# Token halves in the output tiles, gates on a whole bank, and earlier squares and gate logits, in a fused SSM and expert kernel

## The chip, the cores and the metric

The kernel runs on one core of a Trainium2 chip. The metric is the device time of one execution in microseconds; it is read as the median of repeated runs. A separate execution is profiled by the hardware, and its trace gives the views that are quoted here.

## The reference

The output mixes two branches of the same tokens with a gate per token. L is 2048 tokens, D is 576 channels.

```python
x = A_u
g = sigmoid((x * gate_w).sum(-1, keepdims=True))
a = S4(x)      # K[d,l] = Re sum_n C[d,n] exp(dt A l) dt B[d,n]; y = conv(x, K) + x * Dskip
b = PEER(x)    # below
return g * a + (1 - g) * b

# PEER: 32 heads, 64 x 64 = 4096 experts
q  = x @ w_q                                # 32 heads, two halves of 128
s1 = q[..., :128] @ k1.T; s2 = q[..., 128:] @ k2.T   # 64 scores each
# two best of s1 and of s2 give four candidates, the two best of these are the experts
g   = softmax(top_s)                        # over the two
act = gelu(x @ u[top_e])                    # one number per token, head, choice
out = sum over heads and choices of g * act * v[top_e]
```

## The kernel before

**Layout.** The 2048 tokens stand in 16 tiles of 128. The convolution is done by a two-step Fourier transform in matmuls. PEER is done densely: the activations of every token with all 4096 experts are computed (`a` matmuls) and kept in DRAM as `g_d`, and the choice of experts enters as a sparse matrix of gates.

**Stages.** In the *token stage* TensorE computes scores (`s`, from folded keys `whl` and tokens `xb`) and activations (`a`, from `uhl` and `xb`); the taps K of the convolution are generated beside them (`kP` and `kb` matmuls, CS, e, ex and Y on the other engines), and `u_stage1` does the first Fourier step of the tokens (`u` matmuls from `uh`). VectorE takes the best scores from the `s` banks (`m`, `i`). In the *frequency stage* (`freq`), which begins when all taps are stored, `ksb` is loaded, `k_stage1` transforms the taps (`k` matmuls, `k1o`, stored to `sk_d`), `products` multiplies the spectra (`pr`, `pi`, `pv`, `tt`, `vf`, `vo`), and `gating` makes gates and places from the best scores. `v_norm` runs there too: it squares the 32 blocks of value rows for a common scale, and then, in the same loop with the same tiles `vn`, multiplies 16 tiles of tokens by `gate_w` on GpSimd and sums them on ScalarE into the gates `gA`. `v_work` splits the values into f16 high and low parts `vhl` once the scale is known. The *output stage* goes through the 16 tiles in `ORDER` (0, 15, 1, 14, ...).

**One output tile.** `prep` loads the tile's activations from `g_d` in two parts `gl` and puts them through gelu. `onehot` builds, for each of four quarters of the tile's tokens, one-hot matrices `A`, `Be` and the gated `Bg` on VectorE. TensorE multiplies them into banks `S`, and VectorE multiplies `gl` by these banks. The result is split into f16 high and low weights `wh`, and 192 `o` matmuls (32 blocks of experts, three products of high and low parts, two halves of the channels) give the tile's output. `y_part` adds the convolution (`y` matmuls, `ya`); `ya*db` is computed on GpSimd.

**What sets the order.** The program is written by generators under a clock of its own: `clock[0]` counts the matmuls' cost, and each engine has a `free` time that grows by a cost formula per operation. A generator yields until what it needs is ready by that clock (`ready`), or until a buffer is free (`need`, `take`, `free` on tags such as `slot`, `wb`, `sc`). The order in which instructions stand in each engine's queue is thus decided when the program is built, from estimated times; on the chip each engine works through its queue in order and waits for semaphores. Which engine does a split or a copy also follows from the estimated `free` times. All helpers record through one line, so the profile shows L134 for every operation of VectorE, ScalarE and GpSimd, L214 for matmuls and L205 for DMAs on SyncE; the tiles' names tell them apart. The nine buffers `slot` hold `gl` and `wh` in the output stage, 9 KB per partition each.

The lines of `prep` that the prediction's steps concern, with the loads, the four multiplies per quarter, and the weights made at the end:

```python
dma(gl[h], g_d[t][:, 16 * h:16 * h + 16])
...
for h in range(2):
    gv = gl[h].rearrange("p b (r n) -> p b r n", r=2)[:, :, :, n0:n0 + 8]
    V.tensor_tensor(out=gv, in0=pv[:, 16 * h:16 * h + 16], in1=gv, op=OP.mult)
...
yield from split(fl(h[0][:, bs]), fl(h[1][:, bs]), fl(src), s_wg)
```

Of the kernel before, what the change touches and what calls it, by code (L numbers as in the profile page):

```python
# [24 lines left out]
D = 576  # L25
# [113 lines left out]
def body(ctx: ExitStack, tc: tile.TileContext, xT, au, par, logdt, dskip, gatew, wq, kT, uT, vv,  # L139
# [841 lines left out]
    def gating(c):  # L981
# [81 lines left out]
    def u_stage1():  # L1063
# [31 lines left out]
        load(0)  # L1095
        for p in range(NT):
# [4 lines left out]
            h = uf.tile([128, 2, D], F16, tag="uh", name=f"uh{p}", bufs=2)  # L1101
# [22 lines left out]
        while ended[0] < NT:  # L1124
            yield 1
# [139 lines left out]
    def freq():  # L1265
# [14 lines left out]
        spawn(v_norm(), 40)  # L1280
# [115 lines left out]
    def v_norm():  # L1396
        ld = {}

        def load(b):
            a = ff.tile([128, D], F32, tag="vn", name=f"vn{b}", bufs=2)  # L1400
            if b < 32:
                dma(a, vv[128 * b:128 * b + 128])
            else:
                au_load(a, b - 32)
            ld[b] = a
# [3 lines left out]
        for b in range(48):  # L1409
            if b + 1 < 48:  # L1410
                load(b + 1)
            a = ld.pop(b)
            yield from ready(a)
            ju = ff.tile([128, D], BF16, tag="ju", name=f"vj{b}")
            if b < 32:
                S.activation(ju, a, AF.Square, accum_out=vsum[:, b:b + 1])
            else:
                G.tensor_mul(a, a, gw)
                yield from ready(a)
                S.activation(ju, a, AF.Copy, accum_out=gA[:, b - 32:b - 31])  # L1420
            yield 2
            if b != 31:
                continue
            V.tensor_reduce(out=nut[:, 2:3], in_=vsum, axis=AX, op=OP.add)
            yield from ready(nut)
            tag = side()
            yield from need(tag)
            p = bank(tag, "pvn")
            mm(p[:, 0:1], onesb, nut.bitcast(BF16)[:, 5:6], True, True, 0.05)
            yield from ready(p)  # L1430
            sv.extend(root_scale(p[:, 0:1], 1.02))
            free(tag, sv[0])
            vnormed.append(1)
            del p
# [60 lines left out]
    def prep(t):  # L1495
# [9 lines left out]
        yield from ready(*gl)  # L1505
        for h in range(2):
            for b0 in (0, 8):
                g = gl[h][:, b0:b0 + 8]
                S.activation(g, g, AF.Gelu_apprx_tanh)
        for q in range(4):  # L1510
# [20 lines left out]
            del pbs, pS, pv  # L1531
# [4 lines left out]
        h = []  # L1536
        for z in range(2):
            yield from need("slot")
            h.append(slot([32, 128], F16, f"wh{t}_{z}"))
# [300 lines left out]
```

## Time and profile before

| | before |
|---|---|
| median of 3 runs | 1456.58 us (1456.38 to 1456.81) |
| profiled execution | 1458.63 us, its span 1456.8 us, mean granted clock 0.998 |
| busy: PE, DVE, ACT, POOL | 98%, 84%, 53%, 36% of the span |
| last `u` matmul of the token stage | starts at 633.6 us |
| `k` matmuls | 678.7 to 744.2 us |
| products and the transposes of the places | `pv` from 771.3, `tr` to 939.7 us |
| first and last `S` matmul | 954.8 and 1400.0 us |
| first and last `o` matmul | 995.3 and 1452.8 us |

PE is TensorE's matmuls, PEld its weight loads, DVE VectorE, ACT ScalarE, POOL GpSimd and SP SyncE. Busy time of an engine says nothing of what the kernel waits for; that is read from PE's idle time and from who ended it. In the views a row of a group has its count, its busy time, the mean of one in ns, and the idle time of the engine just before it with what ended that; a row of the timeline has start, length, engine, operation and, in brackets, the idle time before it.

### The profile page before, as it was taken

To read this page: it belongs to the slowest core of one execution; us is meant where nothing else is said; L and a number is where in the kernel's file an instruction comes from. 1 tells how busy PE (TensorE), PEld (TensorE's weight loads), DVE (VectorE), ACT (ScalarE), POOL (GpSimd) and SP (SyncE) were. 2 spreads that over 40 slices of the span, in tenths; PEclk is the share of its full clock that TensorE was granted. 3 is DMA by queue.
4 is the path that set the end of the run, shared out by engine and by line. 5 is a ranking of instruction groups with operands and counts; after the bars stand their busy time and mean duration, and the time that the engine had idled before them with its cause. 6 is when DMAs were issued, how large, how long until landed. Compare 5 with 4: busy or idle time off the path is not lost.

```text
span 1456.8 us, 36814 instructions
## 1 busy us (share of the span) xinstructions
PE 1430.8 (98%) x14103; PEld 853.9 (59%) x14105; DVE 1221.0 (84%) x4569; ACT 776.0 (53%) x1304; POOL 521.4 (36%) x510
## 2 busy tenths in 40 slices
PE   7999999999999999999999999999899999999998
PEld 3445445555454445455555444447687887888787
DVE  6898889889877996885989898689998988998860
ACT  6346776796685776834556564576333224323310
POOL 0335357536446446210237999623000100110100
PEclk9999999999999999999999999999999999999999
DMA  8235223442434432269486776787343432342400
GB/s 306 77 112 172 88 80 109 126 138 72 129 106 124 116 104 92 62 211 292 157 304 216 266 250 214 255 265 228 130 122 110 140 120 98 125 148 67 157 9 17
DMA packets 134352, 215.44 MB, mean 148 GB/s; under 512 B 10912, under 2 KB 79904, under 8 KB 127776
## 3 DMA queue, kind: packets, MB, share of 16 engines
q1 hardware_dynamic: 134080, 213.01, 45.3%
q8 instruction: 111, 1.82, 0.5%
q14 instruction: 65, 0.53, 0.1%
q10 hardware_dynamic: 96, 0.07, 0.0%
HBM read 141.74 MB, written 71.30 MB: 146 GB/s over the span
## 4 chain that ended last, share of the span: by engine, by line
PE 85%; DVE 5%; DMA 2%; ACT 1%; issue 0%; POOL 0%; SPq 0%; DVEq 0%; POOLq 0%
PE o L214 25%; PE s L214 22%; PE a L214 22%; PE S L214 4%; PE kb L214 2%; PE wb L214 2%; PE pr L214 2%; DMA vn<-in_au_dram 1%; PE y L214 1%; PE kP L214 1%; PE k L214 1%; DVE i L134 1%; PE pv L214 1%; PE u L214 1%; DVE vhl L134 1%; DVE m L134 1%
## 5 line engine op out<-in xcount | busy, mean ns | idle before, releaser
L214 PE MATMUL o<-vhl,wh 128*128 128x288 f16 x3072 | 389.2, 287 | 0.0
L214 PE MATMUL s<-whl,xb 128*128 128x512 f16 x1536 | 365.0, 379 | 0.0
L214 PE MATMUL a<-xb,uhl 128*128 128x512 f16 x1536 | 359.5, 379 | 0.2 <-DVE go L134 0.2
L214 PEld LDWEIGHTS <-wh 128*128 128x128 f16 x3072 | 296.8, 98 | 77.5 <-issue 3.7
L214 PEld LDWEIGHTS <-xb 128*128 128x128 f16 x1792 | 170.6, 98 | 208.5 <-issue 14.3
L214 PEld LDWEIGHTS <-uhl 128*128 128x128 f16 x1536 | 147.1, 98 | 176.3 <-issue 3.2
L134 DVE FIND_INDEX8 i<-m,s 128x8 uint32<-128x64 f32 x1024 | 206.9, 226 | 0.0
L134 ACT ACTIVATE wh<-gl,s_wg 128x1024 f16<-128x1024 f32 x64 | 69.0, 1137 | 203.6 <-DVE gl L134 203.6
L134 DVE MAX8 m<-s 128x8 f32<-128x64 f32 x1024 | 146.4, 217 | 27.1 <-PE s L214 26.6
L134 POOL TENSOR_TENSOR CS<-CS,ex 128x512 f32<-128x512 f32 x72 | 97.9, 1389 | 147.6 <-DVE ex L134 146.2
L134 POOL TENSOR_TENSOR ya<-ya,db 128x576 f32<-128x576 f32 x16 | 31.8, 1995 | 320.3 <-DVE Bg L134 159.2
L134 ACT ACTIVATE go<-a,i_a 128x512 f32<-128x512 f32 x92 | 61.5, 682 | 89.1 <-PE a L214 63.9
L134 DVE TENSOR_TENSOR gl<-S,gl 128x256 f32<-128x256 f32 x256 | 90.3, 416 | 13.5 <-PE S L214 10.1
L134 POOL TENSOR_TENSOR e<-aN,rt 128x512 f32<-128x512 f32 x72 | 83.1, 1174 | 49.9 <-PE kb L214 43.8
L134 DVE SCALAR_TENSOR_TENSOR wh<-gl,s_wg,wh 128x1024 f16<-128x1024 f32 x64 | 91.1, 1455 | 11.3 <-ACT wh L134 11.3
L134 DVE TENSOR_TENSOR Bg<-Be,vals 128x1024 f16<-128x1024 f16 x128 | 91.7, 758 | 2.2
L134 ACT ACTIVATE gl<-gl 128x1024 f32<-128x1024 f32 x64 | 63.4, 1044 | 34.1 <-DMA gl<-g_d 34.1
L214 PE MATMUL S<-Bg,A 128*128 128x64 f16 x2048 | 73.6, 194 | 6.4 <-DVE Bg L134 6.4
L214 PEld LDWEIGHTS <-A 128*128 128x128 f16 x2048 | 71.4, 98 | 11.4 <-DVE Bg L134 4.9
L134 DVE TENSOR_TENSOR A<-iota_a,vals 128x2048 f16<-128x2048 f16 x64 | 77.9, 1218 | 0.0
L134 DVE MATCH_VALUE_LOAD i<-m,s 128x8 f32 x1024 | 76.3, 75 | 0.1
L214 PE MATMUL s<-wrem,xb 128*128 128x512 f16 x256 | 76.2, 379 | 0.0
(206 smaller groups left out, 2156.6 us busy)
## 6 DMA issues: line engine op xcount, KB each, us to landing
g_d<-go SPq DMA_DIRECT2D x128, 256.0 KB, 2.4
gl<-g_d SPq DMA_DIRECT2D x32, 1024.0 KB, 5.5
wq<-in_wq_dram SPq DMA_DIRECT2D x16, 1152.0 KB, 5.6
su_d<-us SPq DMA_DIRECT2D x32, 288.0 KB, 2.6
sk_d<-k1o SPq DMA_DIRECT2D x32, 288.0 KB, 3.7
vn<-in_vv_dram SPq DMA_DIRECT2D x32, 288.0 KB, 4.1
ui<-su_d SPq DMA_DIRECT2D x16, 576.0 KB, 4.0
ki<-sk_d SPq DMA_DIRECT2D x16, 576.0 KB, 5.5
```

The costliest lines, as they stand in the source:

```text
L134: return f(*a, **k)
L214: T.matmul(o, l, r, start=start, stop=stop)
```

## The change

Four edits are made together.

- A half of a tile is now 64 tokens with all 32 blocks of experts, where it was 128 tokens with 16 blocks. The identity that transposes the places takes its columns in another order, so that quarters 0 and 1 are the first 64 tokens. The load of a half takes 64 of 128 tokens from each row of `g_d`.
- VectorE multiplies `gl` by a whole bank `S` in one instruction of 512 elements, in place of two of 256.
- The weights of a half are made by a generator of its own, `weights`; that of the first half starts after the second quarter.
- `v_norm` keeps only the squares and runs in the token stage, from `u_stage1`, in place, with one buffer; `uh` gets one buffer in place of two. The gate logits become `gate`, which starts 4 us after the frequency stage's loads, where `v_norm` started after 40.

```diff
-                    mm(p[64 * hh:64 * hh + 64, 64 * r:64 * r + 64], x, i[:, 64 * hh:64 * hh + 64], True, True,
-                       0.12 if r == 2 else 0.04)
+                    mm(p[64 * hh:64 * hh + 64, 64 * r:64 * r + 64], x,
+                       i.rearrange("p (h r n) -> p r h n", h=2, r=2)[:, hh], True, True, 0.12 if r == 2 else 0.04)
...
         load(0)
+        spawn(v_norm())
         for p in range(NT):
...
-            h = uf.tile([128, 2, D], F16, tag="uh", name=f"uh{p}", bufs=2)
+            h = uf.tile([128, 2, D], F16, tag="uh", name=f"uh{p}", bufs=1)
...
-        while ended[0] < NT:
+        while ended[0] < NT or not vnormed:
             yield 1
...
-        spawn(v_norm(), 40)
+        spawn(gate(), 4)
         spawn(gating(0), 20)
...
     def v_norm():
+        for b in range(32):
+            a = uf.tile([128, D], F32, tag="vn", name=f"vn{b}", bufs=1)
+            dma(a, vv[128 * b:128 * b + 128])
+            yield from ready(a)
+            S.activation(a, a, AF.Square, accum_out=vsum[:, b:b + 1])
+            yield 9
+        V.tensor_reduce(out=nut[:, 2:3], in_=vsum, axis=AX, op=OP.add)
...
+    def gate():
...
+        for t in range(NT):
+            if t + 1 < NT:
+                load(t + 1)
+            a = ld.pop(t)
             yield from ready(a)
+            ju = ff.tile([128, D], BF16, tag="ju", name=f"gj{t}")
+            G.tensor_mul(a, a, gw)
+            yield from ready(a)
+            S.activation(ju, a, AF.Copy, accum_out=gA[:, t:t + 1])
             yield 2
...
-        gl = [slot([16, 128], F32, f"gl{t}_{h}") for h in range(2)]
+        gl = [slot([32, 64], F32, f"gl{t}_{h}") for h in range(2)]
         for h in range(2):
-            dma(gl[h], g_d[t][:, 16 * h:16 * h + 16])
+            dma(gl[h], g_d[t][:, :, 64 * h:64 * h + 64])
...
+            h = q // 2
             for hb, pS in enumerate(pbs):
-                n0 = 16 * q + 8 * hb
-                pv = pS.rearrange("p (k r b) -> p b r k", r=2, b=32)
-                for h in range(2):
-                    gv = gl[h].rearrange("p b (r n) -> p b r n", r=2)[:, :, :, n0:n0 + 8]
-                    V.tensor_tensor(out=gv, in0=pv[:, 16 * h:16 * h + 16], in1=gv, op=OP.mult)
-                free("wb", *gl)
+                n0 = 16 * (q % 2) + 8 * hb
+                gv = gl[h].rearrange("p b (r n) -> p b r n", r=2)[:, :, :, n0:n0 + 8]
+                V.tensor_tensor(out=gv, in0=pS.rearrange("p (k r b) -> p b r k", r=2, b=32), in1=gv, op=OP.mult)
+                free("wb", gl[h])
...
+            if q == 1:
+                for z in range(2):
+                    yield from need("slot")
+                    wh.append(slot([32, 128], F16, f"wh{t}_{z}"))
+                spawn(weights(t, 0, wh, gl[0]))
...
+        spawn(weights(t, 1, wh, gl[1]))
+
+    def weights(t, h, wh, g):
+        yield from ready(g)
+        for b in (slice(0, 16), slice(16, 32)):
+            hi, lo = (x[:, b, 64 * h:64 * h + 64] for x in wh)
+            src = g[:, b]
...
+                yield from split(hi, lo, src, s_wg)
             yield 0.3
-        free("slot", h[1])
-        free("slot", h[1])
-        st[t] = h
+        free("slot", wh[1])
+        if h:
+            while t not in half:
+                yield 0.3
+            st[t] = wh
+        half.append(t)
```

On VectorE, at the third output tile (the number in a name is a buffer's running number), from `Bg` of its second quarter on. Before, the order of the program is this; behind its last row stand the four multiplies `gl` of the first quarter, then `A`, `Be` and `Bg` of the third.

```order
L134 TENSOR_TENSOR Bg_1_13451<-Be_1_13449,vals 128x1024 x2
L134 SCALAR_TENSOR_TENSOR wh_1_13434<-gl_0_13021,s_wg,wh_0_13433 128x1024
L134 SCALAR_TENSOR_TENSOR vhl_12950<-vhl_12951,sci,vhl_12950 128x576
L134 SCALAR_TENSOR_TENSOR wh_1_13434<-gl_0_13021,s_wg,wh_0_13433 128x1024
L134 SCALAR_TENSOR_TENSOR wh_1_13434<-gl_1_13022,s_wg,wh_0_13433 128x1024
L134 SCALAR_TENSOR_TENSOR vhl_12951<-vs,sci,vhl_12951 128x576
L134 SCALAR_TENSOR_TENSOR ya_13355<-y_0_0_13574,iuk,ya_13355 128x288
L134 SCALAR_TENSOR_TENSOR ya_13355<-y_0_1_13579,iuk,ya_13355 128x288
L134 SCALAR_TENSOR_TENSOR wh_1_13434<-gl_1_13022,s_wg,wh_0_13433 128x1024
L134 SCALAR_TENSOR_TENSOR vhl_12951<-vs,sci,vhl_12951 128x576 x2
L134 SCALAR_TENSOR_TENSOR ya_13360<-y_1_0_13584,iuk,ya_13360 128x288
L134 SCALAR_TENSOR_TENSOR ya_13360<-y_1_1_13589,iuk,ya_13360 128x288
```

After the change the same stretch, up to `Bg` of the third quarter, is this:

```order
L134 TENSOR_TENSOR Bg_1_13402<-Be_1_13400,vals 128x1024 x2
L134 SCALAR_TENSOR_TENSOR vhl_12475<-vs,sci,vhl_12475 128x576
L134 SCALAR_TENSOR_TENSOR wh_1_13219<-gl_1_13002,s_wg,wh_0_13218 128x16x64
L134 SCALAR_TENSOR_TENSOR ya_13366<-y_0_0_13536,iuk,ya_13366 128x288
L134 SCALAR_TENSOR_TENSOR ya_13366<-y_0_1_13541,iuk,ya_13366 128x288
L134 SCALAR_TENSOR_TENSOR ya_13371<-y_1_0_13546,iuk,ya_13371 128x288
L134 SCALAR_TENSOR_TENSOR ya_13371<-y_1_1_13551,iuk,ya_13371 128x288
L134 TENSOR_TENSOR gl_0_13387<-S_0_0_13575,gl_0_13387 128x64x8
L134 TENSOR_TENSOR gl_0_13387<-S_0_1_13592,gl_0_13387 128x64x8
L134 TENSOR_TENSOR A_2_13635<-iota_a,vals 128x2048
L134 TENSOR_TENSOR Be_2_13637<-iota_b,vals 128x1024
L134 TENSOR_TENSOR Bg_2_13639<-Be_2_13637,vals 128x1024 x2
```

One wh and one vhl stand between the two Bg where four of each stood; the other three wh of the tile before are ahead of this stretch.

On ScalarE, in the token stage at the first step of `u_stage1`. Before:

```order
L134 ACTIVATE uh_963<-us,sci 128x576
L134 ACTIVATE go_2_3_1003<-a_2_3_965,i_a 128x512
L134 ACTIVATE vals<-m_0_4_807 128x4x16
L134 ACTIVATE idx<-i_0_4_808 128x4x16
L134 ACTIVATE uhl_893<-us_790,sci 128x512 x2
```

After:

```order
L134 ACTIVATE uh_965<-us,sci 128x576
L134 ACTIVATE vn_918,vsum<-vn_918 128x576
L134 ACTIVATE go_2_3_1006<-a_2_3_967,i_a 128x512
L134 ACTIVATE vals<-m_0_4_807 128x4x16
L134 ACTIVATE idx<-i_0_4_808 128x4x16
L134 ACTIVATE uhl_893<-us_790,sci 128x512 x2
```

A square (`vn`) now stands ahead of the copy of an activation bank (`go`); 32 of them follow each other in this way, the last ahead of the thirteenth of 16 `uh`.

TensorE's instructions are the same in kind, size and number. Between `y` and the third tile's third quarter of `S` its queue has two quarters of `S` and 54 `o` matmuls, where it had 60; the fourth quarter of the second tile stands ahead of the first `o` matmul, where 18 `o` stood ahead of it.

More of the change, by code (lines that the diff above doesn't have):

```diff
@@ L1396, in v_norm @@
     def v_norm():
-        ld = {}
[L1399 to L1405, printed above, removed]
+        for b in range(32):
[4 more added lines that the diff above has]
+            yield 9
@@ new lines, in v_norm, with load @@
+        V.tensor_reduce(out=nut[:, 2:3], in_=vsum, axis=AX, op=OP.add)
+        yield from ready(nut)
+        tag = side()
+        yield from need(tag)
+        p = bank(tag, "pvn")
+        mm(p[:, 0:1], onesb, nut.bitcast(BF16)[:, 5:6], True, True, 0.05)
+        yield from ready(p)
+        sv.extend(root_scale(p[:, 0:1], 1.02))
+        free(tag, sv[0])
+        vnormed.append(1)
+    def gate():
+        ld = {}
+        def load(t):
+            ld[t] = ff.tile([128, D], F32, tag="vn", name=f"xg{t}", bufs=2)
+            au_load(ld[t], t)
@@ L1532, in prep @@
+            del pbs, pS
             if q < 2:
                 oh[q + 2] = onehot(t, q + 2)
+            if q == 1:
[3 more added lines that the diff above has]
+                spawn(weights(t, 0, wh, gl[0]))
         if t != ORDER[-1]:
             spawn(prep(ORDER[ORDER.index(t) + 1]))
[L1536 to L1539, printed above, removed]
@@ L1549, in prep @@
             else:
-                yield from split(fl(h[0][:, bs]), fl(h[1][:, bs]), fl(src), s_wg)
+                yield from split(hi, lo, src, s_wg)
             yield 0.3
-        free("slot", h[1])
-        free("slot", h[1])
-        st[t] = h
+        free("slot", wh[1])
[4 more added lines that the diff above has]
+        half.append(t)
+    half = []
     yt = {}
```

44 lines of the change are left out of this document (8 added, 36 removed).

## The prediction

> **What bounds the kernel now.** I read the page first, then busy time by windows, PE's waits, and the timeline around the one large wait.
>
> ```profile
> PE 1430.8 (98%) x14103; PEld 853.9 (59%) x14105; DVE 1221.0 (84%) x4569; ACT 776.0 (53%) x1304; POOL 521.4 (36%) x510
> ```
>
> PE is busy for 1430.8 us, 98% of the span of 1456.8. The change leaves PE's multiset of instructions as it is, so time can only move in the other 26.0 us, plus what a lower clock costs. The windows say where these lie; a row has the stretch, its length, the busy time of PE, PEld, DVE, ACT and POOL (with counts), the granted clock, the DMA share and GB/s.
>
> ```profile
> 0.00:50.00 50.00, 40.69 (x307) 20.31 (x309) 31.07 (x86) 29.91 (x51) 12.55 (x13) 1.00 0.78 262
> 250.00:300.00 50.00, 50.00 (x544) 25.48 (x543) 41.74 (x126) 36.74 (x56) 31.89 (x26) 1.00 0.42 131
> 450.00:500.00 50.00, 48.35 (x498) 24.01 (x493) 42.57 (x188) 36.10 (x55) 19.73 (x18) 1.00 0.37 111
> 850.00:900.00 50.00, 48.29 (x456) 22.85 (x449) 46.49 (x280) 25.83 (x71) 48.67 (x44) 1.00 0.58 192
> 1000.00:1050.00 50.00, 45.06 (x503) 34.30 (x501) 48.22 (x68) 23.21 (x26) 10.43 (x6) 0.93 0.57 182
> 1150.00:1200.00 50.00, 50.00 (x610) 40.53 (x608) 46.52 (x73) 12.14 (x13) 2.82 (x2) 1.00 0.41 133
> ```
>
> The start loses 9.3 us (50 − 40.69) and the change touches none of it. From 1100 on PE is full although DVE works 46.52 of 50, so cheaper DVE work there buys nothing by itself. The large loss is in 1000 to 1050, where the output tiles begin: PE idles 4.94 us and the granted clock falls.
>
> ```profile
> PE S L214 <- DVE Bg L134: 6.4, 4, 4.6
> PE u L214 <- DVE uh L134: 1.9, 2, 1.4
> PE kb L214 <- issue: 1.6, 1, 1.6
> PE pi L214 <- DVE i L134: 1.3, 1, 1.3
> ```
>
> ```profile
> 1023.00:1028.00 5.00, 0.43 (x4) 0.12 (x3) 4.97 (x11) 0.78 (x1) 0.00 (x0) 0.96 0.96 343
> 1028.00:1032.00 4.00, 3.64 (x40) 2.84 (x41) 3.96 (x8) 0.00 (x0) 0.00 (x0) 0.50 0.43 180
> 1032.00:1036.00 4.00, 4.00 (x27) 2.71 (x24) 3.05 (x8) 0.00 (x0) 0.00 (x0) 0.69 0.00 0
> ```
>
> S matmuls wait for the one-hot product Bg four times, 6.4 us, the longest 4.6. Behind the longest the clock stands at 0.50 for 4 us and 0.69 for 4 us: 4 × 0.50 + 4 × 0.31 = 3.2 us of matmul time. So DVE's lag in this stretch costs 6.4 + 3.2 = 9.6 us.
>
> ```profile
> 1007.72 3.50 DVE L134 TENSOR_TENSOR Bg<-Be,vals 128x1024 f16<-128x1024 f16 x2
> 1008.82 3.67 POOL L134 TENSOR_TENSOR ya<-ya,db 128x576 f32<-128x576 f32 x2
> 1011.83 2.15 PE L214 MATMUL y<-yz,tf 128*32 128x288 f32 x32
> 1018.37 4.25 POOL L134 TENSOR_TENSOR ya<-ya,db 128x576 f32<-128x576 f32 x2 [5.88 <-DMA ya<-in_au_dram]
> 1019.39 3.85 DVE L134 SCALAR_TENSOR_TENSOR vhl<-vs,sci,vhl 128x576 f16<-128x576 f32 x2
> 1027.19 1.29 DVE L134 TENSOR_TENSOR Bg<-Be,vals 128x1024 f16<-128x1024 f16 x2
> 1027.94 0.23 PE L214 MATMUL S<-Bg,A 128*128 128x64 f16 x1 [4.57 <-DVE Bg L134]
> ```
>
> DVE ended Bg of the third tile's second quarter at 1011.2 and of its third quarter at 1028.5: 17.3 us of unbroken work, while PE needed it at 1023.1. Beside POOL's products DVE steps stretch: a pair of Bg takes 3.50 us at 1007.72 and 1.29 at 1027.19.
>
> **The change part by part.** *Gates on a whole bank.* Per tile 16 multiplies of 256 elements become 8 of 512.
>
> ```profile
> L134 DVE TENSOR_TENSOR gl<-S,gl 128x256 f32<-128x256 f32 x256 | 90.3, 416 | 13.5 <-PE S L214 10.1 <-ACT gl L134 3.5
> L134 DVE TENSOR_TENSOR CS<-CS,kP 128x512 f32<-128x512 f32 x19 | 13.1, 687 | 0.7
> L134 DVE SCALAR_TENSOR_TENSOR wh<-gl,s_wg,wh 128x1024 f16<-128x1024 f32 x64 | 91.1, 1455 | 11.3 <-ACT wh L134 11.3
> L134 DVE TENSOR_TENSOR A<-iota_a,vals 128x2048 f16<-128x2048 f16 x64 | 77.9, 1218 | 0.0
> L134 DVE TENSOR_TENSOR Be<-iota_b,vals 128x1024 f16<-128x1024 f16 x64 | 46.2, 721 | 0.0
> L134 DVE TENSOR_TENSOR Bg<-Be,vals 128x1024 f16<-128x1024 f16 x128 | 91.7, 758 | 2.2
> L134 DVE SCALAR_TENSOR_TENSOR ya<-y,iuk,ya 128x288 f32<-128x288 f32 x32 | 15.0, 510 | 0.0
> ```
>
> The nearest 512-element product out of a bank takes 687 ns, so a tile pays 8 × 0.687 = 5.5 instead of 16 × 0.416 = 6.7 us; over 16 tiles DVE loses 18.6 us of work. From 1100 on that lies beside a full PE and is worth nothing; it counts where DVE is late.
>
> *Token halves.* The 192 transposes read the identity's columns in another order, in the same number and size: 0. The weights wh of a half are split after two quarters. Per tile the same four splits run, so their sum stays; they move ahead of the later one-hots. In the new order, between Bg of the third tile's second and third quarters DVE has one vhl, one wh, four ya, two gl, one A, one Be and two Bg: 1.06 + 1.46 + 4 × 0.51 + 2 × 0.69 + 1.22 + 0.72 + 2 × 0.76 = 9.4 us against the 17.3 measured (vhl's mean below). Most of these have room, so what counts is the chain from y on.
>
> ```profile
> 1056.86 3.67 PE o L214 x30
> 1060.53 0.97 PE S L214 x32
> L134 DVE SCALAR_TENSOR_TENSOR vhl<-vhl,sci,vhl 128x576 f16<-128x576 f32 x19 | 19.7, 1060 | 0.8 <-issue 0.8
> ```
>
> An o matmul is 3.67 / 30 = 0.122 us and a quarter of S 0.97. From y's start the new PE order has y (2.1), 12 o, S, 6 o, S, 36 o, then the third quarter: 2.1 + 54 × 0.122 + 2 × 0.97 = 10.6 us. On DVE the first quarter's S ends at 2.1 + 1.5 + 1.0 + about 0.3 = 4.9; two gl (1.4) and A, Be, 2 Bg (3.5) end at 9.8. The four ya end at 4.6 and delay nothing. DVE is ahead by 0.8. Two products of POOL may each stretch a step by 1.1 (3.50 against 1.29 for the pair): then 12.0, a wait of 1.4, and up to 1 us again at the fourth quarter, where 24 o and S (3.9) stand against 4.9 of DVE. So 0 to 2.4 remain; I take 0.8. None comes near the 4.57 that went before the clock's fall, so the 3.2 us of clock go too. The first two tiles, which hold the other S waits, get shorter gl work and no gate product of POOL (next part), so I take all 9.6 off.
>
> *Loads of gates.* A half's load is now 4096 runs of 256 bytes instead of 128 runs of 8 KB.
>
> ```profile
> gl<-g_d SPq DMA_DIRECT2D x32, 1024.0 KB, 5.5
> g_d<-go SPq DMA_DIRECT2D x128, 256.0 KB, 2.4
> DMA to landing us min/median/max: 7.5/8.5/12.4
> L134 POOL TENSOR_TENSOR vn<-vn,gw x16: 1395/1412/1846, 838.7 to 959.4; 128x576 f32<-128x576 f32 x16
> ```
>
> No load of before has runs of 256 bytes. The third row is ksb's: 18 × 128 = 2304 runs of 512 bytes, 1.18 MB, 8.5 us. By bytes a half (1.05 MB) takes 7.6 us at that rate; by runs, (8.5 − 2.4) / (2304 − 512) = 3.4 ns a run (2.4 us and 512 runs are g_d's store), 4096 runs take 2.4 + 3584 × 0.0034 = 14.6. I take 7.6: gl and ksb move 190 and 139 bytes per ns, nearer to each other than their counts of runs (18 fold). What hides it: in the new order a tile's first S stands 84 o or more behind the last S of the tile before, whose end releases the load: 84 × 0.122 = 10.3 us, plus S itself, and now only the first half and its two gelus must be there. Cost 0; without that cover it is a rival below. The Trainium skill, DMA: Bandwidth & Descriptors, Specifications, puts line rate at runs of 512 bytes or more and says that below this the engine does read-modify-write; no run of before shows it.
>
> *Squares and gate logits.* 32 loads and squares of value rows move from 715–835 to the token stage, 16 gate products to the start of the frequency stage.
>
> ```profile
> L134 ACT ACTIVATE vj<-vn 128x576 bf16<-128x576 f32 x48 | 33.1, 689 | 11.2 <-DMA vn<-in_vv_dram 8.9 <-POOL vn L134 2.2
> L134 ACT ACTIVATION_READ_ACCUMULATOR vj<-vn 128x1 f32 x48 | 9.7, 202 | 0.0
> L205 SPq DMA_DIRECT2D vn<-in_au_dram x64: 310/419/2223, 825.6 to 955.7; - x64
> L134 ACT ACTIVATE uh<-us,sci x16: 759/764/785, 92.1 to 626.4; 128x576 f16<-128x576 f32 x16
> L134 ACT ACTIVATE go<-a,i_a 128x512 f32<-128x512 f32 x92 | 61.5, 682 | 89.1 <-PE a L214 63.9 <-issue 22.4 <-DMA g_d<-go 2.3
> ```
>
> ACT gets 32 × (0.689 + 0.202) = 28.5 us between 92 and about 510, some 3.4 per 50 us beside 36.74; the last square stands ahead of the last four uh, so the stage does not wait for it. Each is queued ahead of go, us and the CS steps on ACT; a late load (8.9 us over 8 times, 1.1 each) holds these, and PE through full banks. Bounds: 0, since go already waits for PE 63.9 us, and 12 us if one in three of 32 pays 1.1. I take 0.8. The load of square n+1 on SP waits for square n, 9 us older, so nothing on SP stands behind it. On SP the gates' 64 loads leave 826 to 956 and stand among the stores of the taps' spectrum and of g_d at the start of the frequency stage; each waits for a product two tiles older, and these stores wait behind it. What needs the stores (a ring of three, the products) runs beside s matmuls that fill PE: 0, within the ±1.5 below. One uh buffer instead of two makes ACT wait for u matmuls issued 12 us before: 0. Earlier squares open the vhl work from about 750 instead of 833, but tiles 3 to 7 still wait for their pools: DVE has 13 vhl steps after the products now, 14 before. The gate products (1.41 each on POOL) leave 838 to 961, where POOL was busy 48.67 of 50; PE does not wait for POOL there, so this gives DVE undisturbed steps and nothing of its own. The sigmoid's table load leaves the output start. The waits of pi, u and kb I leave as they are (a shuffle of ±1.5).
>
> **The sum.** −9.6 + 0.8 + 0.8 = −8.0 us. The profiled execution took 1458.63 us, 1.83 around its span and 2.05 above the median 1456.58; the same difference on the median gives 1448.6.
>
> **The rivals.** *The wait stays.* POOL's ya products fall on the third tile's one-hots and DVE is 3 us or more later than reckoned (its backlog of vhl has a margin of about 6 us ahead of y). PE then waits 3 to 4 us again. Whether the clock falls lies between 1.6 us (kb's wait, 1.00 in 450 to 500) and 4.57. By the Trainium skill, TensorE: Matmul & The Clock Gate, Part 1, about 3.4 us of idleness halves it; the 4.57 agrees, and no row shows the border itself. With 3.5 + 3.2 back, 1448.6 − 0.8 + 6.7 = 1454.5, within the bound below. For it: the second pair of ya products began 6.5 us behind y (1018.37 against 1011.83), where the third quarter's one-hots now stand. Against: 9.4 us of work where 17.3 stood.
>
> *The squares hold ACT in the token stage* (the other side): at 12 us or more of late banks, 1448.6 + 11.2 = 1459.8, slower. It decides from about one square in three delaying a go that a bank waits for. Against: ACT has 13 us free in each 50.
>
> *Runs of 256 bytes bound the stage.* A tile takes PE 192 × 0.122 + 4 × 0.97 + half a y, 28.4 us. At 3.4 ns a run, two halves hold the engines 27.9 us per tile; a DMA share of 0.41 is 11.6, of which the old gl loads (2.1 of 3.8 MB at 133 GB/s) were over half, so 5 stay: 33 against 28.4, +4.5 for 14 tiles, some 1510. It decides from (28.4 − 5) / 8192 = 2.9 ns a run. Against: by bytes the same row gives 7.6 us a half. The Trainium skill's rule on short runs, cited above, would have it come out this way.
>
> **How the numbers follow.** A measurement here tells about 0.2% (2.9 us) from no change: 1453.7 to 1459.5 is the same. Forecast 0.72; the wait stays 0.14 (same); squares 0.09 and short runs 0.05 (slower). Predicted 1448.6. Its own range: with the u, kb and pi waits gone too (4.8) and no residue, 1442.2; with 2.4 and 3 us of residue, 1452.4. Reaching into the rival that the wait stays gives 1442.5 to 1457.5.
>
> **What would show it.** Right: no S wait over 1.5 us and clock 1.00 after 1000; gl near 0.69 us; 32 squares before 550 with PE full in 150 to 450; gl landing by 10 us. Wrong: S waiting again near the third tile; PE idle spread over the token stage with ACT named; ACT's gl waiting over 4 us per tile.

## The result and the profile after

The changed kernel takes 1471.69 us (median of 5 runs, 1467.21 to 1473.89) beside 1456.38 of the kernel before (5 runs): ratio 1.0103, 95% interval 1.0085 to 1.0121. It is 15 us slower, where 8 us faster was forecast, and outside the range. The profiled execution is its shortest: 1467.21 us, span 1465.1, 8.3 more than before.

The page's first line, then busy time by windows (columns as in the prediction):

```profile
PE 1432.8 (98%) x14103; PEld 853.4 (58%) x14105; DVE 1214.1 (83%) x4458; ACT 774.6 (53%) x1289; POOL 520.2 (36%) x513
```

```profile
300.00:350.00 50.00, 45.98 (x530) 23.42 (x529) 35.06 (x80) 42.80 (x68) 28.16 (x24) 1.00 0.60 183
650.00:700.00 50.00, 46.16 (x366) 24.11 (x366) 37.98 (x286) 19.31 (x45) 4.91 (x6) 0.97 0.84 274
1000.00:1050.00 50.00, 45.60 (x502) 33.53 (x504) 47.02 (x60) 20.35 (x25) 14.74 (x8) 0.97 0.76 188
1150.00:1200.00 50.00, 50.00 (x618) 40.61 (x616) 47.16 (x62) 18.11 (x18) 3.45 (x2) 1.00 0.54 109
```

Two stretches where PE was full now have holes: 4.02 us in 300 to 350, and 3.84 in 650 to 700 with the clock at 0.97. The hole in 1000 to 1050 is still there (4.40 us, clock 0.97, against 4.94 and 0.93). From 1150 on PE idles 0.3 us in all. PE's waits name the three places (engine, what it waited for: us in all, times, longest):

```profile
PE S L214 <- DVE Bg L134: 4.6, 6, 1.9
PE a L214 <- DVE wrem L134: 3.1, 1, 3.1
PE wn L214 <- ACT k1o L134: 2.0, 1, 2.0
```

The timeline of PE around the S waits:

```profile
1004.24 0.19 PE L214 MATMUL S<-Bg,A 128*128 128x64 f16 x1 [1.15 <-DVE Bg L134]
1004.84 1.09 PE L214 MATMUL S<-Bg,A 128*128 128x64 f16 x31 [0.41 <-DVE Bg L134]
...
1008.97 0.20 PE L214 MATMUL S<-Bg,A 128*128 128x64 f16 x1 [1.95 <-DVE Bg L134]
1009.57 1.10 PE L214 MATMUL S<-Bg,A 128*128 128x64 f16 x31 [0.40 <-DVE Bg L134]
1010.50 17.27 PE L214 MATMUL o<-vhl,wh 128*128 128x288 f16 x126
...
1043.11 1.09 PE L214 MATMUL S<-Bg,A 128*128 128x64 f16 x31 [0.39 <-DVE Bg L134]
```

The third tile, ahead of which the kernel before waits 4.57 us, now waits 0.39. The waits of 1.15 to 1.95 us stand at the second tile's third and fourth quarter, and the 126 o behind them take 17.27 us instead of 15.4 (126 × 0.122), because the clock has dropped.

DVE comes late to these two quarters. Its multiplies and one-hots for them stand behind a copy of an activation bank (`go`), ahead of which it is idle for 4.5 us. SP's steps before that and DVE's copy:

```profile
984.52 4.46 SPq L205 DMA_DIRECT2D gl<-g_d  x2
989.03 6.11 SPq L205 DMA_DIRECT2D g_d<-go  x3
997.67 0.75 DVE L134 TENSOR_SCALAR go<-a,i_a 128x512 f32<-128x512 f32 x1 [4.50 <-issue]
```

The view names nobody who ended this wait ("issue"). The semaphores of the trace do: DVE's queue waits there for the store of `go` that was issued at 989.03, and this store landed at 997.58. On SP it stands behind the two loads of the gates, which hold SP from 984.52 to 988.98. So the waits of the second tile come from the loads in short runs, not from DVE's amount of work.

Groups of instructions, and the load of the gates (us to landing is the last number):

```profile
L134 DVE TENSOR_TENSOR gl<-S,gl 128x512 f32<-128x512 f32 x128 | 82.0, 682 | 30.2 <-ACT gl L134 25.3
gl<-g_d SPq DMA_DIRECT2D x32, 1024.0 KB, 9.4
```

A bookkeeping for all kernels follows. For each window of 50 us the idle time of PE (length less busy time) and the lost clock (length × (1 − granted clock)) are added up by stage, as idle + clock. With 0 to 250 (12.1 to 14.6 in every kernel, not shown) the span less all of it lies between 1429 and 1434 us in 15 of the 16 profiles (1420 in e9, where long idle time and a low clock overlap), so these columns tell differences to some 2 us: of the 8.3 us between the first two rows they hold 5.9. Each profile is one execution; the ratio (with its interval) is against runs of the kernel before on the same chip.

| kernel | median us | ratio (95%) | 250–650 | 650–750 | 750–950 | 950–1150 |
|---|---|---|---|---|---|---|
| before | 1456.4 | | 1.6+0 | 0 | 1.9+0 | 6.4+3.5 |
| changed | 1471.7 | 1.0103 (1.0085–1.0121) | 6.9+0 | 3.8+1.5 | 1.2+0 | 4.4+1.5 |
| e1 halves | 1472.1 | 1.0106 (1.0086–1.0125) | 1.2+0 | 0 | 1.9+0 | 13.2+7.0 |
| e2 squares | 1470.8 | 1.0095 (1.0076–1.0114) | 7.7+3.0 | 0.9+0 | 4.8+1.5 | 4.6+1.5 |
| e3 gates at 40 | 1476.1 | 1.0135 (1.0114–1.0155) | 6.6+3.5 | 1.5+0 | 4.9+1.5 | 8.2+5.0 |
| e4 long runs | 1467.5 | 1.0064 (1.0043–1.0086) | 6.5+3.0 | 3.8+1.5 | 1.1+0 | 2.9+0 |
| e5 halves, long runs | 1467.0 | 1.0067 (1.0052–1.0081) | 1.7+0 | 1.0+0 | 2.0+0 | 8.8+5.0 |
| e6 thin squares | 1469.6 | 1.0085 (1.0070–1.0100) | 6.9+3.5 | 0.9+0 | 4.9+1.5 | 4.6+1.5 |
| e7 loads on ACT | 1476.1 | 1.0128 (1.0110–1.0145) | 6.6+3.5 | 5.7+1.5 | 1.3+0 | 5.8+3.5 |
| e8 gates at 150 | 1472.8 | 1.0113 (1.0093–1.0132) | 6.7+3.5 | 0.8+0 | 0.8+0 | 9.6+5.0 |
| e9 squares per 7 us | 1497.5 | 1.0279 (1.0254–1.0304) | 2.2+0 | 1.8+0 | 3.3+0 | 34.3+18.5 |
| e10 gates at 110 | 1465.7 | 1.0056 (1.0034–1.0078) | 6.5+0 | 0.5+0 | 2.3+1.5 | 5.0+0 |
| e11 thin multiplies | 1463.1 | 1.0039 (1.0024–1.0053) | 2.1+0 | 0.6+0 | 1.9+0 | 6.3+1.5 |
| e12 squares 10, gates 60 | 1480.2 | 1.0157 (1.0132–1.0182) | 18.5+6.5 | 0 | 6.7+1.5 | 3.0+0 |
| e13 late squares | 1461.0 | 1.0015 (1.0003–1.0027) | 1.6+0 | 0.7+0 | 5.0+0 | 4.4+1.5 |
| e14 wrem on DVE | 1477.9 | 1.0124 (1.0104–1.0144) | 1.6+0 | 0 | 7.9+3.5 | 11.1+5.0 |

### The profile page after: what moved, and what is told of

It is laid out like the page before. It is cut to its first block, busy times and chain, and to the rows that moved or that the text cites. A ratio compares the mean times of both kernels' runs of the same rounds, so it can differ in the third digit from the quotient of the medians.

```text
span 1465.1 us, 36622 instructions
## 1 busy us (share of the span) xinstructions
PE 1432.8 (98%) x14103; PEld 853.4 (58%) x14105; DVE 1214.1 (83%) x4458; ACT 774.6 (53%) x1289; POOL 520.2 (36%) x513
## 4 chain that ended last, share of the span: by engine, by line
PE 45%; DVE 5%; DMA 3%; ACT 1%; SPq 1%; issue 0%; DVEq 0%; ACTq 0%
PE o L214 22%; PE s L214 8%; PE a L214 4%; PE S L214 3%; PE pr L214 2%; DMA gl<-g_d 2%; PE pv L214 1%; DVE i L134 1%; PE y L214 1%; PE k L214 1%; SPq L205 1%; DMA wq<-in_wq_dram 1%; DVE m L134 1%; PE wb L214 1%; DVE A L134 1%; DVE gl L134 1%
## 5 line engine op out<-in xcount | busy, mean ns | idle before, releaser
L134 POOL TENSOR_TENSOR ya<-ya,db 128x576 f32<-128x576 f32 x16 | 28.2, 1771 | 320.4 <-DMA ya<-in_au_dram 269.2
L134 ACT ACTIVATE gl<-gl 128x1024 f32<-128x1024 f32 x64 | 64.1, 1049 | 117.1 <-DMA gl<-g_d 103.4
L134 DVE TENSOR_TENSOR gl<-S,gl 128x512 f32<-128x512 f32 x128 | 82.0, 682 | 30.2 <-ACT gl L134 25.3
L134 ACT ACTIVATE go<-a,i_a 128x512 f32<-128x512 f32 x82 | 55.6, 684 | 72.6 <-PE a L214 43.6
L134 DVE SCALAR_TENSOR_TENSOR wh<-gl,s_wg,wh 128x1024 f16<-128x1024 f32 x62 | 78.9, 1296 | 1.3 <-ACT wh L134 1.3
L214 PE MATMUL a<-xb,wrem 128*128 128x512 f16 x256 | 76.1, 379 | 3.7 <-DVE wrem L134 3.1
```

Of the source, the lines that this page charges most:

```text
L134: return f(*a, **k)
L214: T.matmul(o, l, r, start=start, stop=stop)
```

## The experiments

**Each part alone (e1, e2).** e1 takes the squares and gate products back to one loop in the frequency stage and leaves the token halves:

```
-        spawn(v_norm())                  # in u_stage1; uh with bufs=2 again
-        spawn(gate(), 4)
+        spawn(v_norm(), 40)              # the loop of before: squares, then gate products
```

> The output tiles in token halves alone: squares of value rows and gate products stand where the kernel before has them, two uh buffers. Theory A (the loss comes from two places ahead of the output stage: ACT queued behind squares near 305 us of the changed kernel, and SP queued behind the gate rows' loads near 690 us): this kernel has neither place and keeps only what the halves bring, 1452 to 1458 us, and no PE wait over 1.5 us in 100 to 750. Theory B (the gate loads in runs of 256 bytes, landing in 9.4 us instead of 5.5, cost the time in the output stage): 1468 to 1473 us, like the changed kernel.

Measured 1472.06 us: outside Theory A's range and inside Theory B's. The two places are empty, as Theory A said, but the output start is far worse than in either kernel:

```profile
1000.00:1050.00 50.00, 38.87 (x376) 27.89 (x374) 47.60 (x52) 28.48 (x36) 20.63 (x12) 0.86 0.96 228
PE S L214 <- DVE Bg L134: 8.2, 8, 3.7
PE o L214 <- POOL vhl L134: 4.5, 2, 3.8
```

e2 is the kernel before with the squares moved and the gate products in a loop of their own:

```
+        spawn(v_norm())                  # in u_stage1, one square every 9 us; uh with bufs=1
-        spawn(v_norm(), 40)
+        spawn(gate(), 40)
```

> The kernel before with only the 32 squares of value rows moved to the token stage (one uh buffer); the gate products stay at 40 us after the taps' loads, in a loop of their own. Theory A: the token stage loses 4 to 5 us to ACT (a matmul that waits for wrem or for a bank that go has not emptied), and the frequency stage nothing: 1460 to 1463 us. Theory B: 1456 to 1458 us, no loss.

Measured 1470.77: slower by more than Theory A said. The token stage loses 9.1 us more than before the change (7.7 + 3.0 against 1.6), where 4 to 5 were expected, and 750 to 950 loses 4.8 + 1.5, most of it near 770, where wn waits for wj. So each part alone costs 14 to 15 us. Both together cost 15 in the changed kernel and 20 with the gate products at 40, where e2 has them (e3 below): they don't add up, since the output start loses 20.2 us with halves alone and 5.9 in the changed kernel.

**The runs of 256 bytes (e4, e5).** The scratch lies by token half, so a half's load has long runs and the stores get the short ones:

```
-    g_d = dr.tile([NT, 128, 32, 128], F32, name="g_d")
+    g_d = dr.tile([NT * 2, 128, 32, 64], F32, name="g_d")
-            dma(gl[h], g_d[t][:, :, 64 * h:64 * h + 64])
+            dma(gl[h], g_d[2 * t + h])
```

> The changed kernel with the scratch for the gates laid out by token half, so that a half loads as 128 runs of 8192 bytes instead of 4096 of 256 (the stores then have runs of 256 bytes instead of 512). Theory A: gl lands in 5 to 6 us instead of 9.4 and the time stays within 3 us of the changed kernel, 1468 to 1474 us. Theory B: 1455 to 1460 us.

> The output tiles in token halves alone, as in e1, with the scratch for the gates laid out by token half, so that each gl load has 128 runs of 8192 bytes. Theory C (from e1 and e4: a gl load in runs of 256 bytes keeps SP for some 4.5 us, against 0.8 for two loads in long runs, and lands late; behind it stand the loads of vhl, and in front of DVE's gate multiply the gelu that waits for gl): the loss of 950 to 1100 goes and the order of the halves shows what the prediction reckoned for it, 1447 to 1454 us, no o matmul that waits for vhl, and gl landing in 5 to 7.5 us. Rival D (the order of the one-hots, splits and multiplies in halves is itself worse for the third tile): 1464 to 1472 us, as e1.

e4 takes 1467.46 us and e5 1467.0: against the changed kernel and e1 the ratio falls by 0.0039 both times, 5.7 us. Each ratio has an interval of some ±0.002, so the 5.7 is rough. In both pairs every engine does the same steps in the same order, so the 5.7 us are what short runs cost on the loads, less what they cost on the stores, and no change of order is in them. e4 ends just under Theory A's range and far from B's: the short runs are a part of the loss, not the cause. e5 lies in Rival D's range, though 5 us under e1: its output start loses 13.8 us instead of 20.2, where C's total needed less than the 9.9 of the kernel before. SP's queue shows part of the way. First the changed kernel at the first tile's gates, then e4 (start, length, SP's steps):

```profile
953.48 4.52 SPq L205 DMA_DIRECT2D gl<-g_d  x2
958.04 4.75 SPq L205 DMA_DIRECT2D vhl<-in_vv_dram  x1
```

```profile
959.26 0.81 SPq L205 DMA_DIRECT2D gl<-g_d  x2
960.12 0.43 SPq L205 DMA_DIRECT2D vhl<-in_vv_dram  x1
```

Two loads in short runs keep SP 4.52 us, and the load of vhl behind them takes 4.75 instead of 0.43. Their landing falls from 9.4 us to a median of 7.3 (row of gl's tile in e4), not to the 5 to 6 expected:

```profile
DMA to landing us min/median/max: 4.7/7.3/10.9
```

At the second tile the queue does it. e4's rows where the changed kernel's DVE stood idle for 4.5 us:

```profile
987.70 0.81 SPq L205 DMA_DIRECT2D gl<-g_d  x2
996.92 0.75 DVE L134 TENSOR_SCALAR go<-a,i_a 128x512 f32<-128x512 f32 x1 [0.71 <-PE a L214]
```

By the trace, the store of `go` that DVE needs is issued 0.86 us after the loads begin instead of 4.51, and takes about as long to land (8.2 us instead of 8.6). PE's S waits at the output start fall from 4.6 us to 1.4. At the other places the queue and the landing were not separated.

**The token stage (e6, and 250 to 650 in e9 and e14).** e6 is e2 with narrow squares in the same order:

```
-            S.activation(a, a, AF.Square, accum_out=vsum[:, b:b + 1])
+            nc.scalar.activation(a[:, :16], a[:, :16], AF.Square, scale=6.0, accum_out=vsum[:, b:b + 1])
```

> As e2, the squares alone in the token stage, in the same order on every engine, but each square covers 16 of the 576 columns (scaled so that the sum has about its size); the scale of the values is then only roughly that of the reference. It takes away most of the 0.68 us that a square holds ACT; the loads of its rows, the reading of the sum (0.19 us) and the order stay. Theory A (ACT's time is what the token stage lacks): the wait for wrem near 305 us falls below 1.5 us and the one near 485 below 1: 1464 to 1466 us against 1470.8 of e2. Rival E (the shift of the order does it, a group's wrem now stands behind a run of cosine and exponential steps on ACT): the waits stay, 1469 to 1472 us.

Measured 1469.62, Rival E. The order is that of e2 on every engine. A square now holds ACT 0.21 us instead of 0.68, and the wait for wrem is longer, if anything (3.6 us against 3.1 in e2):

```profile
L1399 ACT ACTIVATE vn<-vn x32: 198/206/219, 93.2 to 514.5; 128x16 f32<-128x16 f32 x32
...
PE a L214 <- DVE wrem L134: 3.6, 1, 3.6
```

So not ACT's time but the shifted order does it. In the changed kernel, ACT's rows ahead of the waiting matmul, and the last of DVE's, are these:

```profile
300.05 1.28 ACT L134 ACT_TABLE_LOAD   x1
301.34 1.15 ACT L134 ACTIVATE CS<-CS,halfpi 128x1024 f32<-128x1024 f32 x1
...
304.38 1.04 ACT L134 ACTIVATE CS<-CS 128x1024 f32<-128x1024 f32 x1
305.33 0.70 ACT L134 ACTIVATE wrem<-ur,sci 128x512 f16<-128x512 f32 x1
...
308.78 0.74 DVE L134 SCALAR_TENSOR_TENSOR wrem<-ur,sci,wrem 64x512 f16<-64x512 f32 x1
```

A group's wrem stands behind a table load and four steps of CS, and its second half on DVE (308.78) behind two rounds of Y and two e, which need those CS, and two copies. ACT works without a wait from 290 to 306, so no late load of a square is in it. e9, with a square every 7 us instead of 9, has the squares denser and no such wait: 2.2 us lost in 250 to 650. e14 makes wrem on DVE:

```
         if c:
-            S.activation(rem[:, 0, :], r, AF.Copy, scale=s)
+            V.tensor_scalar(rem[:, 0, :], r, s, None, op0=OP.mult)
```

> e4 with the high half of each group's remainder (wrem, 8 steps of 0.7 us) made on DVE instead of ACT. Theory E (wrem stands behind a run of cosine steps on ACT, where the plan thought ACT free): the wait of 3.1 us near 305 us falls below 1. If it stays, the matmul waits for something else than ACT's order. The shift also moves the output start: the count gives PE 6.0 us less than DVE there (2.4 more in e4), so 4 to 10 us more are lost in 950 to 1050, and the total is 1468 to 1476 us.

The wait is gone (1.6 us lost in 250 to 650, as before the change). The total of 1477.88 is a little above the expectation (by the ratio, 1.0124 × 1456.4 = 1474.4, it is inside); the new order loses 16.1 us at the output start and 11.4 in 750 to 950.

**The gate products (e3, e7, e8).** e3 and e8 change the number in `spawn(gate(), 4)` to 40 and (on e4) to 150; e7 issues the gate rows' loads on ACT's queue:

```
-            au_load(ld[t], t)
+            for d, o in au_rows(au, t, ld[t]):
+                dma(o, d, nc.scalar)
```

> The changed kernel with the gate products started 40 us after the taps' loads, as the kernel before starts them, instead of 4. Theory A: the wait of PE near 690 us (3.8 us of idle time and 1.5 of a lower clock in the changed kernel) goes, since the 16 loads of gate rows no longer stand ahead of the stores of the taps' spectrum on SP: 1464 to 1467 us against 1471.7 of the changed kernel. Theory B: 1471 to 1473 us.

> The changed kernel with the 64 loads of gate rows issued on ACT's queue instead of SP's, in the same order otherwise. Theory A (SP's queue: these loads wait in order for a gate product two tiles older, and stores of the taps' spectrum and the loads of wq wait behind them): PE's idle time in 650 to 700 falls from 3.8 to under 1.2 us and its clock stays at 1.00: 1465 to 1468 us against 1471.7. Rival F (the products and sums on POOL and ACT do it, not the loads): no change there, 1470 to 1474 us. [...]

> e4 (the changed kernel with the scratch by token half) with the gate products started 150 us after the taps' loads, about where the kernel before has them, behind the last loads of wq. Theory A: the idle time near 690 (3.8 us and 1.5 of clock) goes and nothing takes its place; what stays is the token stage's: 1459 to 1463 us against 1467.5 of e4. Rival F: it moves to another place, 1465 to 1470 us.

e8 against e4 is the cleanest pair: up to 680 us they do the same. With the products at 4, SP's queue (the changed kernel) and DVE's and ACT's waits in 675 to 695 read:

```profile
678.83 0.42 SPq L205 DMA_DIRECT2D gw<-in_gatew_dram  x1
679.30 9.01 SPq L205 DMA_DIRECT2D xg<-in_au_dram  x8
688.41 0.40 SPq L205 DMA_DIRECT2D g_d<-go  x1
688.90 5.43 SPq L205 DMA_DIRECT2D sk_d<-k1o  x7
```

```profile
ACT k1o L134 <- DMA sk_d<-k1o: 2.3, 2, 2.1
DVE k1o L134 <- DMA sk_d<-k1o: 6.0, 3, 5.4
```

The eight loads of gate rows take SP 9.0 us; the stores of the taps' spectrum start behind them, copies into k1o wait for these stores, and PE for the copies. What slows the eight loads isn't shown: a product it is not, since POOL's first begins at 689.35, behind all eight. In e8 the stretch holds no xg row, and the loss falls from 3.8 + 1.5 to 0.8. On ACT's queue (e7) the loss stays, at 5.7 + 1.5, and ACT itself now stands behind a load:

```profile
ACT go L134 <- DMA xg<-in_au_dram: 11.5, 1, 11.5
```

So e7 does not tell the queue from the products, and e8 moves both. That the loads are the way is read from the rows of SP and the waits for the stores; no run separates it. What the gates don't cost there they cost later: at 40 (e3) the loads stand ahead of the last loads of wq and the loss is 4.9 + 1.5 in 750 to 950; at 150 (e8) the output start loses 9.6 + 5.0. All three totals came out above what either theory said, since each new order opened waits elsewhere.

**The output start (e9 to e12).** The count is the one of the expectations: PE's work between the first S of the first tile and the S of the third tile's third quarter, less DVE's steps between the Bg of the same quarters, both from the order and the durations of single steps; an estimate, in us. e9 changes `yield 9` to `yield 7` in the squares, e10 the gates' start to 110, e12 both to 10 and 60 (all on e4). e11 is e5 with, for the first three tiles:

```
-                V.tensor_tensor(out=gv, in0=pv, in1=gv, op=OP.mult)
+                nc.vector.tensor_tensor(out=gv[:, :8], in0=pv[:, :8], in1=gv[:, :8], op=OP.mult)
```

> e4 with a square of value rows every 7 us instead of 9 in the token stage. On every engine the order shifts: a count of the matmuls between the first S and the S of the third tile's third quarter, at 0.216 us for an a matmul, 0.122 for o and 0.97 for a quarter of S, gives PE 35.5 us of work here, against 67.7 in e4, since the last a matmuls are done earlier; DVE's steps up to that quarter's Bg are the same 64.5. Theory G (the output start is decided by how much other matmul work stands between the quarters of S while DVE makes its one-hots): PE waits some 25 us in 950 to 1050 and the kernel takes 1480 to 1492 us. Rival (the work before and behind evens out, and the loss follows the loads or the squares): within 5 us of e4, 1463 to 1472. In the token stage: if the wait for wrem near 305 us is a coincidence of the order, it goes or moves; if it is the load on ACT, it stays over 3 us.

> e4 with the gate products started 110 us after the taps' loads, between e4 (4) and e8 (150). By the count of e9's text PE has 67.2 us up to the third tile's third quarter and DVE 68.2: 1.0 short, where e4 has 2.4 to spare and e8 lacks 2.9. Theory A with G: the idle time near 690 is below 1.2 us, no wait for wj near 750 (the last wq loads stand ahead), the output start loses 3 to 6 us: 1461 to 1466 us. Rival: the gate products on POOL and their loads cost the same wherever they stand: 1467 to 1473 us.

> e5 (token halves alone, long runs) in the same order, but the gate multiplies of the first three tiles cover a quarter of their elements, so DVE has some 0.5 us less in each of the ten that stand up to the third tile's third quarter, 5 us of the 6.1 that it is short there; the rest of those gates stays unmultiplied, so the first three output tiles are not the reference's. Theory G: the idle time of 950 to 1050 falls from 8.8 us (and 5.0 of clock) to under 5 (and under 2): 1458 to 1462 us against 1467.0. Rival (POOL's steps that stretch the one-hots, and late vhl, not DVE's amount of work): it stays above 7.5 us, 1465 to 1468.

> e4 with a square every 10 us and the gate products started 60 us after the taps' loads. The count gives PE 0.5 us less than DVE up to the third tile's third quarter. Theories A and G: the wait near 690 us goes; some 1 to 5 us near 750 may take its place, since the loads of wq still stand behind gate rows there; the output start loses 3 to 6 us; the wait for wrem near 305 us goes if it was a coincidence: 1458 to 1466 us. Rival: 1467 to 1473 us, each of the losses found again.

e9 took 1497.54 us, 5 more than Theory G's upper end. Its window and PE's rows at the third tile's place:

```profile
1000.00:1050.00 50.00, 29.73 (x362) 22.37 (x363) 43.34 (x53) 23.56 (x29) 17.48 (x10) 0.75 0.71 238
...
1011.93 1.14 PE L214 MATMUL o<-vhl,wh 128*128 128x288 f16 x4 [15.64 <-ACT wh L134]
...
1041.69 0.20 PE L214 MATMUL S<-Bg,A 128*128 128x64 f16 x1 [4.67 <-DVE Bg L134]
```

The a matmuls ran out, and PE waits 15.64 us for the first tile's weights. Ordered by the count (PE's work less DVE's), the kernels in halves with long runs lose in 950 to 1150: e9 (−29.0) 34.3+18.5; e5 (−6.1) 8.8+5.0; e14 (−6.0) 11.1+5.0; e8 (−2.9) 9.6+5.0; e13 (−2.5) 4.4+1.5; e10 (−1.0) 5.0+0; e12 (−0.5) 3.0+0; e4 (+2.4, by the figures of e9's text +3.2) 2.9+0. The kernel before, with its 16 multiplies per tile, is no member of this list: it counts −15.7 and loses 6.4+3.5. PE's S waits alone are 16.4, 6.2, 5.2, 9.6, 1.8, 2.6, 0.8 and 1.4 us in this order: kernels that lack 2.9 us or more wait over 5 us, the others under 3. The zero of the count is not sharp (with each step's mean duration from the traces all eight lie 4 to 9 us lower, in the same order), and it holds no DMA: in e13, e10, e12 and e4 1.5 to 2.6 us of the loss is PE's wait for the table tf ahead of y. e11, with e5's order on every engine, took 1463.11 us; the idle time of 950 to 1150 fell from 8.8 to 6.3 and the clock's loss from 5.0 to 1.5. That lies between G (idle time under 5) and the rival (over 7.5). The waits for vhl (2.5 us) stayed, so DVE's amount of work is a part of it and not all. e10 and e12 behave at the output start as counted. In total e10 met its expectation, e12 missed it by 14 us: its token stage lost 25 us at other places (kb 9.1, wb 3.3, wrem 2.5).

**All three causes away (e13).** Halves with long runs, squares back in the frequency stage, gates at 110:

```
-        spawn(v_norm(), 40)
+        spawn(gate(), 110)
+        spawn(v_norm(), 40)              # the squares alone, one buffer, uh with bufs=2
```

> Token halves with the scratch by token half, the squares of value rows back in the frequency stage (40 us after the taps' loads, one buffer) and the gate products in a loop of their own 110 us after them, so between the changed kernel's place and that of before. The count gives PE 2.5 us less than DVE up to the third tile's third quarter (e10: 1.0 less). Theory H (the squares' harm is that they shift the order of the token stage, the gates' that their loads stand ahead of the taps' stores, the halves' that the output start lacks cover and its loads have short runs; without all three what the prediction wanted is left): no PE wait over 1.5 us in 250 to 700, output start 5 to 8 us with little loss of clock against 6.4 and 3.5 of before: 1453 to 1459 us, no slower than before. Rival I (any new order loses some 8 us somewhere, since the kernel before was picked among many orders): 1462 to 1470 us, with waits over 2 us at places that none of the kernels had yet.

Measured 1460.95 us, ratio 1.0015 (1.0003 to 1.0027): of 15 us some 2 are left. That is Theory H but for those 2 us, and its range stood on 1456.5 for the kernel before, which took 1458.88 among these runs. It is one order, though, and spacings alone move the total by 30 us (e4 and e9), so a further cause that this order happens to hide is not ruled out. PE's S waits are down to 1.8 us in all, and nothing is gained over before, since other places took the time:

```profile
PE y L214 <- DMA tf<-in_tf_dram: 2.6, 1, 2.6
PE S L214 <- DVE Bg L134: 1.8, 3, 1.2
PE pv L214 <- ACT tt L134: 1.6, 1, 1.6
```

No version tried beats the kernel before.

## Why the prediction was wrong

- **The S waits, −9.6 + 0.8.** The mechanism was right for the third tile: 0.39 us where 4.57 stood, beside a residue of 0.8 forecast. The step that failed is "The first two tiles, which hold the other S waits, get shorter gl work ... so I take all 9.6 off". Before, the first tile held 1.0 us of them and the second none. Now the second has 3.9 us, so 4.4+1.5 are left of 6.4+3.5: −4.0 instead of −8.8. They came by way of the next term: DVE was idle 4.5 us for a store behind the loads of gates, and with long runs (e4) 2.9+0 are left. Work was counted for the third tile alone, and nothing was counted that DVE's other steps wait for. With halves alone (e1) even the third tile fails: it waits 6.4 us.
- **Loads of gates, 0.** The landing of 9.4 us lay between the 7.6 that was taken and the 14.6 by runs. The step that failed is "What hides it": the cover was reckoned for the gelus that need the gates, not for what stands behind the loads on SP, which they hold 4.5 us a pair. Cost 5.7 us by e4 and e5, of which the term above already has 3.0 (5.9 lost at the output start against e4's 2.9). The rival of 1510 us didn't come: from 1150 on PE is full. The Trainium skill, DMA: Bandwidth & Descriptors, Specifications, has line rate only from 512 bytes on; the direction agrees, but with e4's stores in 256-byte runs instead the time falls, so here it mattered on which transfers the short runs lie.
- **Squares, +0.8.** The step that failed is the price of late loads, "Bounds: 0 ... and 12 us ... I take 0.8". The loss was 5.3 (6.9 in 250 to 650 against 1.6), so the rival that squares hold ACT had the direction, but not the mechanism: e6 takes ACT's time away and the loss stays; another spacing (e9) or another engine for wrem (e14) removes this wait. A step's cost was summed where its shift of the order was what counted.
- **Gate products moved, 0.** "What needs the stores ... runs beside s matmuls that fill PE: 0" failed: 3.8+1.5 us near 690. The queue was named and its waiters too; that the taps' ring of stores and the k matmuls have less slack than the 9 us of loads was not worked out. The loads that did it did not wait for a product two tiles older, as the prediction has it, but stood first in the loop.
- **What was right:** gl's multiply (0.682 us against 0.69), DVE's relief being worth nothing from 1150 on, 32 squares ahead of 550. Of the signs, PE full in 150 to 450, no S wait over 1.5 us (1.95) and a clock of 1.00 after 1000 failed, and the sign for short runs spoke: ACT's gl waits 103.4 us over 16 tiles, 6.5 each, where over 4 was to be read as wrong (idle time ahead of gl's steps: us, times):

```profile
its engine sat idle before it (us, times) until:
  DVE gl L134: 137.7, 28
  DMA gl<-g_d: 103.4, 25
```

- **The shuffle, ±1.5.** Far too small: the order is planned anew over the whole program, and spacings of the squares alone move the total by 30 us (e4 and e9).
- **In sum**, the columns of the profiled executions give −4.0 + 5.3 + 5.3 (near 690) − 0.7 (750 to 950) = 5.9 of the 8.3 us. The rest of the 15 us has two sides: the kernel before was profiled 2.2 us above its median, and the changed one in the shortest of its five runs, 4.5 below. In that run the clock held through the wait at 305 us; in five other profiles with that wait it did not (below), for 1.5 to 3.5 us. The mean clock of the four longer runs is 0.995, 0.997, 0.997 and 0.998 against its 0.998; that they are longer for this reason is argued, not shown.

## What to carry to other kernels

Where a planner lays out the program, an edit's price is the new order: count, for each place where one engine hands to another, the work on both sides from the new order over every tile, not only where the old wait was. Work that is finished earlier can take away the cover under which the next stage hides. A transfer in short runs is to be priced by what stands behind it in its queue as well as by its landing. An experiment that keeps the order on every engine (e4, e5, e6, e11 against their partners) tells a cause; one that moves it shows the cause and a new order at once.

## What the hardware showed

The same wait of PE, 3.09 us for wrem just behind one of 0.63, left the clock alone in two profiles (changed, e10) and lowered it in five (e2, e3, e4, e7, e8). PE's rows in the changed kernel, and two windows of 3.41 us over the waits:

```profile
306.09 0.39 PE L214 MATMUL a<-xb,wrem 128*128 128x512 f16 x1 [0.63 <-ACT wrem L134]
309.57 0.39 PE L214 MATMUL a<-xb,wrem 128*128 128x512 f16 x1 [3.09 <-DVE wrem L134]
...
304.24:307.65 3.41, 1.61 (x7) 0.46 (x5) 3.20 (x5) 3.38 (x5) 0.00 (x0) 1.00 0.92 275
307.65:311.07 3.42, 1.50 (x7) 0.70 (x8) 2.62 (x6) 3.40 (x5) 2.13 (x2) 1.00 0.36 148
```

The same in e3:

```profile
309.76 0.61 PE L214 MATMUL a<-xb,wrem 128*128 128x512 f16 x1 [3.09 <-DVE wrem L134]
...
304.72:308.13 3.41, 1.32 (x6) 0.30 (x4) 3.20 (x5) 3.38 (x4) 0.00 (x0) 1.00 1.01 315
308.13:311.54 3.41, 1.78 (x5) 0.68 (x6) 2.33 (x6) 3.39 (x5) 2.41 (x2) 0.50 0.26 108
```

The windows are not chosen freely. Within a trace the low clock (0.50) starts on a grid of 3.413 us and lasts 3.41 us or a multiple of it, save where the span ends: in the changed kernel it starts at 693.36 and 1010.80, which lie 93.0 × 3.413 apart, and lasts 3.41 each time; in e3 it lasts 6.83 from 308.13. Counted on this grid from 11 us on, the 16 profiles have 60 windows at full clock that the low clock follows. Every window with less than 1.4 us of matmuls is among them, none with more than 1.65 is, and between the two both happen (with 1.50 us the clock held in the changed kernel and fell in e8). So where a wait falls on the grid decides, and the grid lies elsewhere in each execution: the same 3.7 us of idle time cost nothing more in two profiles and 1.5 to 3.5 us of clock in five. The Trainium skill, TensorE: Matmul & The Clock Gate, Part 1, has a window of about 3.4 us that runs freely, and half the clock after an idle one. Length and free run agree with these traces; that the window must be idle does not, since windows with up to 1.65 us of matmuls lowered the clock here.
